# Four row blocks of a weight product in split float32r, and GpSimd taking over subtractions and integer additions of a weight conversion

## The chip, the cores and the metric

One core of one Trainium2 chip. The metric is device time in microseconds (us) of one execution. Before the change three runs took 500.30, 500.75 and 500.87 us, with a median of 500.75. TensorE multiplies matrices into PSUM; VectorE (DVE), ScalarE (ACT) and GpSimd (POOL) work elementwise; SyncE (SP) issues most of the DMAs. Each has its own queue of instructions, kept in order.

## The reference

For 8 batches and 8 heads, `x` has 512 rows of 64 and `state` 32 rows of 64. Attention goes both ways:

```python
scores = scale * x @ state.T          # per head, 512 x 32
xread  = softmax(scores) @ state      # 512 x 64
scores2 = scale * state @ x.T         # 32 x 512
sread  = softmax(scores2) @ x         # 32 x 64
y = concat([xread, sread], rows)      # 544 rows per batch, heads side by side: 512 columns
out = ((y @ w1) * (y @ w2)) @ w3 @ w_out
```

w1 and w2 are 512 x 1024, w3 is 1024 x 1024, w_out 1024 x 512. The weights come as float64, the result is float32.

## The kernel before

**Algebra.** The kernel never forms xread. It multiplies the state by w1 and w2 once per batch ("sw", line 146 through `per_head`) and the transposed softmax by that (`stage1`, line 306), takes the product of the two results (`hidden`), and multiplies by `wo` = w3 @ w_out (`stage2`, through `project`, line 316), which is computed once at the start. Products that must keep float32's accuracy in the float32r type are made from split parts: `split` (lines 93 to 98) makes a high part, a ScalarE copy to float32r, and a low part, a VectorE subtraction; three products (high by low, high by high, low by high) make one.

**The weights.** They lie in DRAM as the bits of float64. `to_f32` (lines 101 to 135) turns one piece of 128 x 1024 into float32 in two halves with a `yield` between them: it loads the 1 MB piece into `raw` (three buffers, line 113); ScalarE makes the value from the high words (line 117) and `ulps`, the rounding part, from the low words (line 125; for the first two pieces VectorE does this, line 121; two buffers); after the `yield` VectorE shifts the bits (line 129) and adds `ulps` as an integer (line 133). There are 20 pieces: eight "chunks" `w34_k` (a row of w_out, 512 columns, and half a row of w3), four rows of w3 (`w3t`, rows 4 to 7; two buffers `w3`), and eight "halves" of w1 and w2 (`w12`, `convert_half`, numbers 0 to 7).

**w3 @ w_out.** Row blocks 0 to 3 of `wo` are accumulated in float32 while the chunks come in (`w34_first`, line 389). Blocks 4 to 7 follow, in float32 too, from the w3 rows (`w34`, line 402): eight matmuls each, each of which is two instructions in the trace. `finish` splits a block into `wo` high and low.

**Order.** Up to `order.close()` (line 461) ScalarE and VectorE keep the order in which the code is written, TensorE and SP always do; behind it a planner orders ScalarE and VectorE. In this first stretch the order is: all eight chunks and w3 rows 4 and 5 with `w34_first`; `load_x(0)`, the scores of batch 0 (line 146 with `x_d`); then block 4, the softmax of batch 0 in steps (`go(softmax)`) between the conversions of halves 0 and 1 (w1_0, w2_0), w3 rows 6 and 7, halves 2 and 3 (w1_1, w2_1); blocks 5 and 6; `sets(0)` (sw of batch 0, first quarter, needs halves 0 and 1); five matmuls of block 7; `sets(1)` (needs halves 2 and 3); the rest of block 7. Then `stage1` of batch 0 runs; halves 4 to 7 are converted beside it, and `sw_steps(0)[2:]` needs them, after the third `stage1`. From there on each batch repeats the same work.

```python
        for k in range(FT + AHEAD):
            run([partial(convert_first, k) if k < FT else partial(convert_w3, k - FT // 2)])
            if k >= AHEAD:
                w34_first(k - AHEAD)
        load_x(0)
```

The rows of w_out in float32 lie in the places of halves 4 to 7 (`places`), so before, a half from 4 on can't be written until block 7 has read them. The low words' name inside `to_f32` is set in line 116:

```python
            high, low = words[:, 1], words[:, 0]
```

GpSimd has nothing in this kernel but four one-element memsets of the launch.

Of the kernel before, what the change touches and what calls it, by code (L numbers as in the profile page):

```python
# [22 lines left out]
F32 = mybir.dt.float32  # L23
# [4 lines left out]
ALU = mybir.AluOpType  # L28
AX = mybir.AxisListType
P = 128  # L30
NF = 512
NW = 1024
AHEAD = 2
LAST = 5
PARTS = {0: (640, 1024), 1: (512, 1024)}
WARM = 15

@with_exitstack
def attn_bilinear_kernel(
# [10 lines left out]
    nc = tc.nc  # L50
    B, _, NT, H, D = x_s.shape
# [4 lines left out]
    FT, DO = w34_k.shape[0], out.shape[2]  # L56
# [30 lines left out]
    def bank():  # L87
        return ps_o.tile([P, NF], F32, name="ps_o")

    def two_banks():  # L90
        return ps_2.tile([P, 2, NF], F32, name="ps_2")

    def split(hi, lo, src):

        return (
            nc.scalar.copy(out=hi, in_=src),  # L96
            nc.vector.tensor_tensor(out=lo, in0=src, in1=hi.bitcast(F32), op=ALU.subtract),  # L97
        )


    def to_f32(pool, src, out, ends=(NW,), loads=(), wout=None):

        raw = pool.tile([P, NW], mybir.dt.int64, name="raw", bufs=3)
        ulps = pool.tile([P, NW], I32, name="ulps", bufs=2)  # L110
        parts = [slice(*ends) for ends in zip((0, *ends), ends)]
        for start, stop in zip((0, *loads), (*loads, NW)):
            nc.sync.dma_start(out=raw[:, start:stop], in_=src[:, start:stop])
        for part in parts:
            words = raw[:, part].bitcast(I32).rearrange("p (n k) -> p k n", k=2)
            high, low = words[:, 1], words[:, 0]
            nc.scalar.activation(  # L117
                out=out[:, part], in_=high.bitcast(F32), func=AF.Prelu, scale=2.0**-112, alpha=-(2.0**32)
            )
            if len(parts) > 1:  # L120
                nc.vector.tensor_scalar(
                    out=ulps[:, part], in0=low.bitcast(U32), scalar1=2.0**-29, scalar2=None, op0=ALU.mult
                )
            else:
                nc.scalar.activation(out=ulps[:, part], in_=low.bitcast(U32), func=AF.Copy, scale=2.0**-29)  # L125
        yield
        for part in parts:
            bits = out[:, part].bitcast(I32)
            nc.vector.tensor_scalar(out=bits, in0=bits, scalar1=3, scalar2=None, op0=ALU.logical_shift_left)
            for dest, start, stop in ((wout, 0, DO), (out, DO, NW)) if wout is not None else ((out, 0, NW),):  # L130
                piece = slice(max(start, part.start), min(stop, part.stop))
                if piece.start < piece.stop:
                    nc.vector.tensor_tensor(  # L133
                        out=dest[:, piece].bitcast(I32), in0=out[:, piece].bitcast(I32), in1=ulps[:, piece], op=ALU.add
                    )

# [37 lines left out]
    def attention_steps(b):  # L174
# [3 lines left out]
        def scores():  # L178
# [6 lines left out]
            s1 = work_tile()  # L185
            nc.vector.transpose(out=flat(s1), in_=flat(ps))

            m2 = att.tile([P, KT], F32, name="m2")
            nc.vector.tensor_reduce(out=m2, in_=ps, axis=AX.X, op=ALU.max)
            nc.vector.tensor_scalar_mul(m2, m2, -SCALE)  # L190
# [3 lines left out]
            for kt in range(KT):  # L194
# [65 lines left out]
    def sw_pair():  # L260
        return [main.tile([P, KT, NF], F32R, name=f"sw_{part}", bufs=2 * HALF) for part in ("hi", "lo")]
# [32 lines left out]
    def new_g():  # L294
        return [main.tile([P, NF], F32R, name=f"g_{part}", bufs=FT) for part in ("hi", "lo")]
# [37 lines left out]
    reads = {}  # L333
# [21 lines left out]
    def run(steps):  # L355
        for step in steps:
            for _ in step() or ():
                pass
# [12 lines left out]
    with tc.tile_pool(name="pro", bufs=2) as pro:  # L371
# [7 lines left out]
        def finish(i):  # L379
            split(wo["hi"][:, i], wo["lo"][:, i], w34_ps[i][:, :DO])  # L380

        def convert_first(k):
            ends = PARTS.get(k, (NW,))
            return to_f32(pro, w34_k[k], chunks[k], ends, (), wout=w_out[k])

        def w34_first(k):

            for i in range(FT // 2):
                nc.tensor.matmul(  # L389
                    w34_ps[i][:, :DO], chunks[k][:, DO + i * P:DO + (i + 1) * P], w_out[k],  # L390
                    start=(k == 0), stop=(k == FT - 1),
                )

        def convert_w3(i):
            w3s[i] = pro.tile([P, NW], F32, name="w3", bufs=2)
            return to_f32(pro, w3t[i - FT // 2], w3s[i])

        def w34(i, ks=range(FT)):
            if ks[0] == 0:
                w34_ps[i] = bank()  # L400
            for k in ks:
                nc.tensor.matmul(  # L402
                    w34_ps[i][:, :DO], w3s[i][:, k * P:(k + 1) * P], w_out[k], start=(k == 0), stop=(k == FT - 1)
                )

        def convert_half(n):

            return to_f32(pro, w12[n], places[n])

        def sets(quarter):  # L410
            for i in range(2):
                sw_quarter(0, quarter, i)
# [9 lines left out]
                    project(acc[tt], gs, tt, ft)  # L422

        order = ctx.enter_context(ExitStack())
        order.enter_context(tc.manual_schedule(engines={mybir.EngineType.Activation, mybir.EngineType.DVE}))
        pair = two_banks()
        w34_ps.update(enumerate([bank(), bank(), pair[:, 0], pair[:, 1]]))
        for k in range(FT + AHEAD):
            run([partial(convert_first, k) if k < FT else partial(convert_w3, k - FT // 2)])
            if k >= AHEAD:  # L430
                w34_first(k - AHEAD)
        load_x(0)
        scores, reads[0], _ = attention_steps(0)
        softmax = scores()
        next(softmax)
        finish(0)
        finish(1)
        split(wo["hi"][:, 2:4], wo["lo"][:, 2:4], pair[:, :, :DO])
        w34(4)

        w1_0, w2_0, w1_1, w2_1 = map(convert_half, range(4))
        go = lambda steps: next(steps, None)
        w3_6 = convert_w3(6)
        go(w1_0), go(softmax), go(w1_0)
        finish(4)
        go(w2_0), go(w3_6), go(softmax), go(w3_6)
        w34(5)
        go(softmax)
        go(w2_0)
        finish(5)  # L450
        w3_7 = convert_w3(7)
        go(w3_7), go(w3_7), go(w1_1), go(w1_1), go(w2_1), go(w2_1)
# [118 lines left out]
```

## Time and profile before

| | us |
|---|---|
| median of three runs | 500.75 |
| span of the profiled execution | 498.4 |
| around that span, against the median | 2.35 |
| TensorE busy | 492.3 |
| VectorE busy | 285.7 |
| ScalarE busy | 219.3 |
| GpSimd busy | 0.2 |

The profiled execution has no time of its own beside its span; the runs' median stands for it. A row of a group reads: line, engine, operation, output <- inputs, shapes, count, then busy time and mean of one in ns, then idle time ahead of them and what ended it. A row of the order of time reads: start, length, engine, line, operation, and in brackets the idle time before it and its releaser. A row of the chain reads: start, length, engine, tile and line.

### The profile page before, as it was taken

What the parts mean: (1) busy time and instruction counts of PE and PEld (TensorE: products, weight loads), DVE (VectorE), ACT (ScalarE), POOL (GpSimd) and SP (SyncE); (2) the same over time, 40 slices, a digit from 0 to 9 for tenths busy, and PEclk for the clock granted to TensorE, in tenths of its full rate; (3) what the DMA queues carried; (4) which work ended last, traced back from release to release, by engine and by line L of the source; (5) the groups of instructions that cost most, each with busy time, mean ns of one, the idle gap of its engine ahead of it and who ended that gap; (6) DMA issues with size and microseconds to landing.
All of it is one profiled execution on the core that took longest, in us unless ns stands there. A gap on an engine that the chain in (4) does not pass through costs nothing.

```text
span 498.4 us, 7562 instructions
## 1 busy us (share of the span) xinstructions
PE 492.3 (99%) x3054; PEld 362.8 (73%) x3054; DVE 285.7 (57%) x394; ACT 219.3 (44%) x325; POOL 0.2 (0%) x4
## 2 busy tenths in 40 slices
PE   8999999999999999999999999999999999999996
PEld 6444467767867886788678867886788678888885
DVE  5669896772539343934393539354934493530780
ACT  4777884443444244334333434243424342431650
POOL 0000000000000000000000000000000000000000
PEclk9999999999999999999999999999999999999999
DMA  8996962013400350035003500350035003301001
GB/s 343 364 380 237 364 264 33 11 47 80 181 22 19 79 189 23 20 79 188 21 27 76 185 22 27 77 184 22 26 78 183 22 26 78 93 24 49 21 1 42
DMA packets 52323, 52.41 MB, mean 105 GB/s; under 512 B 42304, under 2 KB 43328, under 8 KB 47680
## 3 DMA queue, kind: packets, MB, share of 16 engines
q1 hardware_dynamic: 47488, 43.27, 26.3%
q10 hardware_dynamic: 4800, 8.65, 4.6%
q8 instruction: 24, 0.39, 0.3%
q14 instruction: 11, 0.09, 0.1%
HBM read 38.27 MB, written 8.91 MB: 95 GB/s over the span
## 4 chain that ended last, share of the span: by engine, by line
PE 95%; DVE 2%; ACT 2%; DMA 1%; issue 0%; DVEq 0%
PE ps_o L316 38%; PE ps L306 35%; PE ps L146 7%; PE ps L507 3%; PE ps_o L402 3%; PE ps_o L389 3%; PE ps L389 3%; PE ps L508 2%; PE ps_o L242 1%; DMA raw<-in_w_k_dram 1%; ACT ulps L125 0%; ACT w_sb L117 0%; ACT wo_hi L96 0%; DVE w L133 0%; DVE work L204 0%; DVE wo_lo L97 0%
## 5 line engine op out<-in xcount | busy, mean ns | idle before, releaser
L316 PE MATMUL ps_o<-wo_lo,g_hi 128*128 128x512 f32 x272 | 107.0, 394 | 0.0
L316 PE MATMUL ps_o<-wo_hi,g_hi 128*128 128x512 f32 x272 | 106.0, 390 | 0.0
L316 PE MATMUL ps_o<-wo_hi,g_lo 128*128 128x512 f32 x272 | 105.9, 389 | 0.0
L306 PE MATMUL ps<-at_lo,sw_hi 128*128 128x512 f32 x256 | 100.1, 391 | 0.0
L306 PE MATMUL ps<-at_hi,sw_lo 128*128 128x512 f32 x256 | 99.6, 389 | 0.0
L306 PE MATMUL ps<-at_hi,sw_hi 128*128 128x512 f32 x256 | 99.6, 389 | 0.0
L291 DVE TENSOR_TENSOR tmp<-tmp,ps 128x512 f32<-128x512 f32 x64 | 43.9, 687 | 77.0 <-ACT tmp L290 76.9
L97 DVE TENSOR_TENSOR g_lo<-tmp,g_hi 128x512 fp32r<-128x512 f32 (+1 forms) x72 | 47.5, 661 | 41.7 <-ACT g_hi L96 41.6
L96 ACT CAST g_hi<-tmp 128x512 fp32r<-128x512 f32 (+1 forms) x72 | 43.1, 599 | 53.6 <-DVE tmp L291 48.8
L290 ACT COPY tmp<-ps 128x512 f32<-128x512 f32 x64 | 37.7, 589 | 62.8 <-PE ps L306 52.2
L316 PEld LDWEIGHTS ps_o<-wo_lo,g_hi 128*128 128x128 f32 x272 | 51.0, 188 | 18.0 <-issue 7.5
L316 PEld LDWEIGHTS ps_o<-wo_hi,g_lo 128*128 128x128 f32 x272 | 51.1, 188 | 10.8
L316 PEld LDWEIGHTS ps_o<-wo_hi,g_hi 128*128 128x128 f32 x272 | 51.1, 188 | 10.3
L97 DVE TENSOR_TENSOR sw_lo<-ps,sw_hi 128x1024 fp32r<-128x1024 f32 (+1 forms) x34 | 38.4, 1155 | 32.8 <-ACT sw_hi L96 32.8
L306 PEld LDWEIGHTS ps<-at_lo,sw_hi 128*128 128x128 f32 x256 | 48.1, 188 | 10.9 <-issue 1.1
L306 PEld LDWEIGHTS ps<-at_hi,sw_hi 128*128 128x128 f32 x256 | 48.1, 188 | 10.2 <-issue 0.2
L306 PEld LDWEIGHTS ps<-at_hi,sw_lo 128*128 128x128 f32 x256 | 48.1, 188 | 10.0
L329 ACT COPY tmp<-ps_o 128x512 f32<-128x512 f32 x34 | 19.8, 583 | 76.1 <-PE ps_o L316 76.1
L96 ACT CAST sw_hi<-ps 128x1024 fp32r<-128x1024 f32 (+1 forms) x34 | 31.7, 967 | 14.3 <-PE ps L146 14.2
L146 PE MATMUL ps<-w_sb,st 64*32 64x512 f32 (+1 forms) x544 | 31.6, 572 | 0.0
L402 PE MATMUL ps_o<-w_sb,w 128*128 128x512 f32 x64 | 28.5, 599 | 0.1
L402 PEld LDWEIGHTS ps_o<-w_sb,w 128*128 128x128 f32 x64 | 11.8, 190 | 15.9 <-issue 13.8
(65 smaller groups left out, 417.9 us busy)
## 6 DMA issues: line engine op xcount, KB each, us to landing
raw<-in_w_k_dram SPq DMA_DIRECT2D x8, 1024.0 KB, 6.6
x_d<-in_x_d_dram SPq DMA_DIRECT2D x8, 1024.0 KB, 7.1
raw<-in_w_dram SPq DMA_DIRECT2D x8, 1024.0 KB, 6.3
x_s<-in_x_s_dram SPq DMA_DIRECT2D x8, 1024.0 KB, 5.4
out_dram<-tmp ACTq DMA_DIRECT2D x32, 256.0 KB, 2.0
raw<-in_w3t_dram SPq DMA_DIRECT2D x4, 1024.0 KB, 7.2
a_t<-work SPq DMA_DIRECT2D x96, 32.0 KB, 1.9
sread<-turned SPq DMA_DIRECT2D x128, 4.0 KB, 1.7
```

The costliest lines, as they stand in the source:

```text
L96: nc.scalar.copy(out=hi, in_=src),
L97: nc.vector.tensor_tensor(out=lo, in0=src, in1=hi.bitcast(F32), op=ALU.subtract),
L146: nc.tensor.matmul(ps[j * NS:(j + 1) * NS, q], sts[b][rows, j], moving(rows, j), start=True, stop=True)
L290: nc.scalar.copy(out=a_sb[:, :n], in_=ps[:, 0, :n])
L291: nc.vector.tensor_tensor(out=a_sb[:, :n], in0=a_sb[:, :n], in1=ps[:, 1, :n], op=ALU.mult)
L306: nc.tensor.matmul(ps[:, i], w[:, kt, c:c + P], a[:, kt], start=(k == 0), stop=(k == 3 * KT - 1))
L316: nc.tensor.matmul(ps[:, :DO], g, wo[w][:, ft, :], start=(ft == 0 and k == 0), stop=(ft == FT - 1 and k == 2))
L329: stored[:] = [nc.scalar.copy(out=o, in_=ps[:, :DO])]
L389: nc.tensor.matmul(w34_ps[i][:, :DO], chunks[k][:, DO + i * P:DO + (i + 1) * P], w_out[k], start=(k == 0), stop=(k == FT - 1),)
L402: nc.tensor.matmul(w34_ps[i][:, :DO], w3s[i][:, k * P:(k + 1) * P], w_out[k], start=(k == 0), stop=(k == FT - 1))
L507: nc.tensor.matmul(ps[:, i], wh[:, ks], sr[:, kt], start=(kt == 0), stop=False)
L508: nc.tensor.matmul(ps[:, i, :n], wl[:, ks], sr[:, kt, 1], start=False, stop=(kt == NP - 1))
```

## The change

- Blocks 4 to 7 of w3 @ w_out are computed in float32r from split parts: `split_w_out` and `split_w3` make the high parts on ScalarE and the low parts on GpSimd; `w34` issues 24 matmuls a block, first the 16 with the high part of w3, then the 8 with the low part. The parts of w_out lie in the `g` buffers, those of w3 in the `sw` buffers, both unused at that time.
- Blocks 4 and 5 accumulate in a pair of PSUM banks and are split together.
- The integer additions of all eight halves of w1 and w2 go to GpSimd (`add=nc.gpsimd`).
- `to_f32` has a parameter `low` and a test on it, given by `convert_half`.
- x of batch 0 is loaded behind chunk 4; its scores stand on TensorE behind the fourth `w34_first`, and two more `yield`s let the steps of its softmax stand between the chunks.
- GpSimd keeps the written order in the first stretch too, and that order is new.

```diff
-LAST = 5
+X_BEHIND = 4
-    def to_f32(pool, src, out, ends=(NW,), loads=(), wout=None):
+    def to_f32(pool, src, out, ends=(NW,), loads=(), wout=None, add=nc.vector, low=nc.scalar):
...
-            if len(parts) > 1:
+            if low is nc.vector or len(parts) > 1:
                 nc.vector.tensor_scalar(
                     out=ulps[:, part], in0=low.bitcast(U32), scalar1=2.0**-29, scalar2=None, op0=ALU.mult
                 )
...
-                    nc.vector.tensor_tensor(
+                    add.tensor_tensor(
                         out=dest[:, piece].bitcast(I32), in0=out[:, piece].bitcast(I32), in1=ulps[:, piece], op=ALU.add
                     )
...
             nc.vector.transpose(out=flat(s1), in_=flat(ps))
+            if b == 0:
+                yield
...
+            if b == 0:
+                yield
             J = KT * S // NS
...
+        w_out_parts, w3_parts = {}, {}
+
+        def split_w_out(k):
+            hi, lo = w_out_parts[k] = new_g()
+            nc.scalar.copy(out=hi, in_=w_out[k])
+            nc.gpsimd.tensor_tensor(out=lo, in0=w_out[k], in1=hi.bitcast(F32), op=ALU.subtract)
+
+        def split_w3(i):
+            w3_parts[i] = [t.rearrange("p k f -> p (k f)") for t in sw_pair()]
+            hi, lo = w3_parts[i]
+            nc.scalar.copy(out=hi, in_=w3s[i])
+            nc.gpsimd.tensor_tensor(out=lo, in0=w3s[i], in1=hi.bitcast(F32), op=ALU.subtract)
...
+        def w34_terms(i):
+            hi, lo = w3_parts[i]
+            for k in range(FT):
+                for w, part in ((hi, 1), (hi, 0)):
+                    yield w[:, k * P:(k + 1) * P], w_out_parts[k][part]
+            for k in range(FT):
+                yield lo[:, k * P:(k + 1) * P], w_out_parts[k][0]
+
+        def w34(i, first=0, last=3 * FT):
+            if first == 0:
+                w34_ps[i] = bank() if i > 5 else later[:, i % 2]
+            for n, (w, moved) in enumerate(w34_terms(i)):
+                if first <= n < last:
+                    nc.tensor.matmul(
+                        w34_ps[i][:, :DO], w, moved, start=(n == 0), stop=(n == 3 * FT - 1)
+                    )
...
-            return to_f32(pro, w12[n], places[n])
+            return to_f32(pro, w12[n], places[n], add=nc.gpsimd, low=nc.vector if n < 4 else nc.scalar)
...
+        for k in range(FT):
+            chunk = convert_first(k)
+            go(chunk)
+            if k == X_BEHIND:
+                load_x(0)
+            if k:
+                split_w_out(k - 1)
+            if k == X_BEHIND + 1:
+                w34_first(k - AHEAD)
+                scores, reads[0], _ = attention_steps(0)
+                softmax = scores()
+                go(softmax), go(softmax)
+            elif k >= AHEAD:
+                w34_first(k - AHEAD)
+            if k == X_BEHIND + 2:
+                go(softmax)
+            go(chunk)
+        w34_first(FT - 2)
+        w34_first(FT - 1)
+        w3_4, w3_5, w3_6, w3_7 = map(convert_w3, range(FT // 2, FT))
+        w1_0, w2_0, w1_1, w2_1 = map(convert_half, range(4))
+        go(w3_4)
+        split_w_out(FT - 1)
+        go(softmax)
+        go(w3_4)
+        split_w3(4)
+        later = two_banks()
+        w34(4)
+        go(w3_5), go(softmax), go(w3_5)
         finish(0)
         finish(1)
         split(wo["hi"][:, 2:4], wo["lo"][:, 2:4], pair[:, :, :DO])
+        split_w3(5)
         w34(5)
+        go(w3_6), go(w3_6), go(w3_7)
+        split_w3(6)
+        go(w3_7)
+        go(w1_0), go(w1_0), go(w2_0), go(w2_0)
+        split_w3(7)
+        split(wo["hi"][:, 4:6], wo["lo"][:, 4:6], later[:, :, :DO])
         go(softmax)
+        go(w1_1), go(w1_1), go(w2_1), go(w2_1)
         load_tokens(0)
         w34(6)
+        w34(7, 0, 2 * FT)
         sets(0)
         finish(6)
-        w34(7, range(LAST))
+        w34(7, 2 * FT)
         sets(1)
-        w34(7, range(LAST, FT))
         finish(7)
```

More of the change, by code (lines that the diff above doesn't have):

```diff
@@ L424, in attn_bilinear_kernel @@
         order = ctx.enter_context(ExitStack())
-        order.enter_context(tc.manual_schedule(engines={mybir.EngineType.Activation, mybir.EngineType.DVE}))
+        order.enter_context(tc.manual_schedule(
+            engines={mybir.EngineType.Activation, mybir.EngineType.DVE, mybir.EngineType.Pool}
+        ))
+        go = lambda steps: next(steps, None)
         pair = two_banks()
         w34_ps.update(enumerate([bank(), bank(), pair[:, 0], pair[:, 1]]))
-        for k in range(FT + AHEAD):
-            run([partial(convert_first, k) if k < FT else partial(convert_w3, k - FT // 2)])
-            if k >= AHEAD:
-                w34_first(k - AHEAD)
[L432 to L435, printed above, removed]
+        for k in range(FT):
[6 more added lines that the diff above has]
+            if k == X_BEHIND + 1:
+                w34_first(k - AHEAD)
+                scores, reads[0], _ = attention_steps(0)
[18 more added lines that the diff above has]
+        go(w3_5), go(softmax), go(w3_5)
         finish(0)
```

20 lines of the change are left out of this document (1 added, 19 removed).

## The prediction

> **What bounds the kernel now.** I read the page's first part, then the chain that ended last, then the order of time on single engines in the first 78 us, where every edit lies.
>
> ```profile
> span 498.4 us, 7562 instructions
> PE 492.3 (99%) x3054; PEld 362.8 (73%) x3054; DVE 285.7 (57%) x394; ACT 219.3 (44%) x325; POOL 0.2 (0%) x4
> ```
>
> TensorE (PE) is busy for 99% of the span, so a change pays only by what it takes from TensorE, and costs whatever TensorE then has to wait. The chain of work that ended last, in order of time (start, length, what), shows the stretch that changes:
>
> ```profile
> 35.88 1.02 ACT wo_hi L96
> ...
> 50.84 7.13 PE ps_o L402 x16
> 57.98 1.02 PE ps L146 x32
> 59.00 4.49 PE ps_o L402 x10
> 63.49 1.02 PE ps L146 x32
> 64.52 2.77 PE ps_o L402 x6
> 67.29 8.18 PE ps L306 x36
> 75.47 1.88 PE ps L146 x32
> ...
> 119.45 21.76 PE ps L306 x96
> ```
>
> From 50.84 us the chain runs on TensorE without a break. Two places of it are gates: line 146 at 57.98 and 63.49 (sets(0), sets(1)) needs halves 0 to 3 of w1 and w2 converted, and line 146 at 75.47 needs halves 4 to 7. After 75.47 nothing is changed but order, and that part is TensorE's throughout, so the time moves by as much as the start of that group moves.
>
> How near are the other engines? The windows give, for each stretch: its bounds, its length, busy time and count of PE, weight loads, VectorE (DVE), ScalarE (ACT) and GpSimd (POOL), the granted clock, the share of DMA and GB/s.
>
> ```profile
> 8.00:34.00 26.00, 26.00 (x61) 11.26 (x62) 17.93 (x29) 18.85 (x19) 0.00 (x0) 1.00 0.98 372
> 34.00:72.20 38.20, 38.15 (x172) 17.90 (x171) 35.35 (x44) 30.84 (x39) 0.00 (x0) 1.00 0.81 320
> ```
>
> VectorE is busy for 35.35 of 38.20 us and ScalarE for 30.84. Both end just ahead of the gate:
>
> ```profile
> 71.01 1.15 ACT L125 ACTIVATE ulps<-raw 128x1024 int32<-128x1024 uint32 x1
> 72.03 0.60 ACT L290 COPY tmp<-ps 128x512 f32<-128x512 f32 x1
> ...
> 72.76 1.23 DVE L133 CUSTOM_DVE_ANT_0 w_sb<-w_sb,ulps 128x2048 uint16<-128x2048 uint16 x1
> ```
>
> The last addition of half 7 ends at 72.76 + 1.23 = 73.99, only 1.5 us ahead of 75.47. The conversion is thus a second chain, nearly as long as TensorE's, and it decides what a shorter TensorE is worth.
>
> **The change part by part.** *TensorE.* Four rows of w3 @ w_out go from float32 to three float32r products.
>
> ```profile
> 36.80 21.18 PE L402 MATMUL ps_o<-w_sb,w 128*128 128x512 f32 x48
> ```
>
> That is 48 instructions, and with the 10 and 6 of the chain 64, in 21.18 + 4.49 + 2.77 = 28.4 us. In their place stand 4 x 24 = 96 float32r matmuls of the shape of line 306, of which the chain has 96 in 21.76 us. **Removed: 28.4 - 21.8 = 6.6 us.** Were nothing else late, the gate at 75.47 would be reached at 68.9. Batch 0's scores on TensorE (16 matmuls, about 1.0 us) only move.
>
> *ScalarE.* It gets eight copies of w_out rows and four of w3 rows, and gives back next to nothing.
>
> ```profile
> L125 ACT ACTIVATE ulps<-raw 128x1024 int32<-128x1024 uint32 x11 | 12.7, 1156 | 0.0
> L96 ACT CAST wo_hi<-ps_o 128x512 fp32r<-128x512 f32 x6 | 3.4, 586 | 0.0
> L196 ACT ACTIVATE e<-ps,m 128x512 f32<-128x512 f32 x2 | 1.4, 684 | 1.6 <-DVE m L190 1.6
> L207 ACT ACTIVATE work<-work 128x1024 f32<-128x1024 f32 x1 | 1.1, 1061 | 0.9 <-DVE work L204 0.9
> L96 ACT CAST at_hi<-work 128x1024 fp32r<-128x1024 f32 x1 | 1.0, 1047 | 3.3 <-DVE work L220 3.3
> L96 ACT CAST wo_hi<-ps 128x1024 fp32r<-128x1024 f32 x1 | 1.0, 1013 | 0.8 <-PE ps L389 0.8
> ```
>
> A copy of 512 costs 3.4 / 6 = 0.57, one of 1024 1.0 us: 8 x 0.57 + 4 x 1.0 = 8.6 us more on ScalarE. The diff also hands the low words of halves 0 to 3 to VectorE by a parameter `low`. But line 116, which the diff leaves, gives the name `low` to the low words in each part before the test `low is nc.vector` is reached. So the test is false, and the 4 x 12.7 / 11 = 4.6 us of those line-125 operations stay on ScalarE. What this says of the title's low parts touches only these; the low parts of the float32r splits do go to GpSimd.
>
> *Before 34 us* ScalarE has 26.00 - 18.85 = 7.2 us idle; seven of the copies and the two exponentials of scores2 (4.0 + 1.4 = 5.4 us) fit in. The 1 MB load of x_d goes ahead of chunks 5 to 9 in SP's queue: at 372 GB/s it puts each off by 2.8 us. In VectorE's queue the transpose of the scores (1.24 us) now stands ahead of chunk 5's shift and waits for TensorE; chunk 5 to 7's additions and TensorE's first half wait behind it. Chunk 7 is ready at 28.35 and wanted at 32.25, and 1.0 us later with the scores in front:
>
> ```profile
> 27.06 1.29 DVE L133 CUSTOM_DVE_ANT_0 w_sb<-w_sb,ulps 128x1024 uint16<-128x1024 uint16 x2 [0.37 <-ACT ulps L125]
> ...
> 32.25 1.88 PE L389 MATMUL ps_o<-w_sb 128*128 128x512 f32 x4
> ```
>
> Slack 3.9 + 1.0 = 4.9 against 2.8 + 1.2 + 1.2 (a reduction) = 5.2 us. I cost it at nothing; the early lead covers it, and without cover it is 0.3 us.
>
> *From 34 us on ScalarE*: 30.84 - 1.4 (exponentials gone ahead) + 4.0 + 0.6 = 34.0 us of work. Without a wait it ends at 68.0, with the waits of before less the exponentials' (38.20 - 30.84 - 1.6 = 5.8) at 73.8.
>
> *GpSimd.* No operation of this size stands in the trace of before; its four instructions are memsets of one element:
>
> ```profile
> L556 POOL MEMSET const-float32-1.0<- 128x1 f32 x1 | 0.1, 100 | 0.0
> ```
>
> The nearest rows are VectorE's groups from 48 to 75.5 us:
>
> ```profile
> L97 DVE TENSOR_TENSOR at_lo<-work,at_hi 128x1024 fp32r<-128x1024 f32 x1 | 1.2, 1225 | 1.1 <-ACT at_hi L96 1.1
> L97 DVE TENSOR_TENSOR g_lo<-tmp,g_hi 128x512 fp32r<-128x512 f32 x1 | 0.7, 693 | 0.1
> L129 DVE TENSOR_SCALAR w_sb<-w_sb 128x1024 int32<-128x1024 int32 x7 | 4.8, 686 | 0.0
> ```
>
> Low end: GpSimd is as fast as VectorE, 1.2 us for 1024. High end: it reads its operands one after the other and waits for one VectorE operation besides, 2.5 + 1.2 = 3.7 us. From the two VectorE rows an operation has 0.16 us of start and 0.53 us for 512 elements; two passes over 1024 are 0.16 + 4 x 0.53 = **2.3 us**, over 512 1.2 us. I take these, since two inputs on one path are the plainest reason for a slower engine; both ends stay for the range. The Trainium skill, "GPSIMD Engine Reference", section 3.1 "Elementwise — side-by-side cycle accounting", has 4497 ns against VectorE's 2293 for an addition of 2048 elements: an estimate by that ratio is 2.4 us and a sum 1.3 us higher than the one below; no run here shows it.
>
> GpSimd gets, from 34 us on, one low part of w_out (1.2), four of w3 and eight integer additions: 1.2 + 12 x 2.3 = 28.8 us. VectorE loses eight additions, 8 x 1.23 = 9.8 us. New waits: ScalarE's low words of a half need the `ulps` buffer that GpSimd's addition two halves back has to leave (two buffers), and all of ScalarE's later splits are queued behind; the conversion of w3 row 6 (two `w3` buffers) waits in the same way for GpSimd's low part of row 4. The sums of rows 4 and 5 move to the third pair of PSUM banks, and sets(0) takes the first pair, which the copy at 35.88 leaves 20 us ahead of need: no cost.
>
> *Do the two engines run side by side?* This is the term that decides. The shift of line 129 takes 0.69 us for 1024 elements where a two-operand subtraction takes 1.23: it runs at double rate, with one operand. Both kinds so draw two streams at a time from SBUF. If GpSimd reads over the second of those paths, it and these VectorE operations take turns. From 34 us VectorE still has 12 shifts (8.3), four additions for w3 (4.9), the subtraction, product and low part of the softmax (3.7) and two g_lo (1.4): 18.3 us. **Taking turns: 34.0 + 28.8 + 18.3 = 81.1 us** for half 7, against the 75.4 at which the gate opens now: +5.7 us, and the 6.6 us on TensorE become waits ahead of line 146. At 2.0 us an operation it is +2.0, at 2.7 +10.7, at the high end of 3.7 +23, at 1.2 nothing is lost by it.
>
> The Trainium skill, "SBUF — State Buffer", section "SBUF: two separate sides", says that the port pair is an exclusive lock held for a whole instruction, against VectorE operations in a two-port mode or with two SBUF inputs; it speaks against this change. No row of before has both engines at work, so the trace neither agrees nor disagrees yet.
>
> **Forecast**, taking turns: the span goes from 498.4 to 504.1, and the median 500.75, which has 2.35 us more around that span, to **506.4 us**.
>
> **The rivals.** *Side by side, ScalarE last.* ScalarE ends half 7 at 73.8, GpSimd adds 2.3 us: 76.1 against 75.4, +0.7: 501.4 us. For it: GpSimd's own 28.8 us fit into 38. Against it: nothing but the argument on the paths. Spread 499.7 to 503.
>
> *Faster: the waits of ScalarE close.* Of its 7.4 us of waits in the window 3.3 are for one transpose (line 220) behind other work on VectorE, which now has eight additions less. If all close and the engines run side by side, half 7 is done at 68.0 + 2.3 = 70.3 and the gate opens 5.1 us earlier; if half of them close, 73.2: 2.2 us earlier, 498.5 us. It decides as soon as half 7 is added before 75.4 minus 1, so with a GpSimd operation below 2.3 us and under 4 us of ScalarE waits. Against it: in the new order the low part of w3 row 7 stands between the additions of halves 1 and 2, and the transpose of at behind the split of wo rows 4 and 5. Should my reading of `low` be wrong, ScalarE loses 4.6 us and this case is the likely one: about 497.
>
> *The edit does nothing for the end:* the gains on TensorE are eaten in the first half by late chunks and stay even there, within 1 us of before. That lies inside the side-by-side case.
>
> **How the numbers follow.** Taking turns 0.55, all of it slower by over 0.2%; side by side with ScalarE last 0.27 (same 0.17, slower 0.07, faster 0.03); faster 0.18. That is faster 0.21, same 0.17, slower 0.62; 0.2%, 1.0 us, is about what a measurement of this kernel can tell from no change. Cases of both signs hold chances, so: taking turns by itself spans 502.8 (2.0 us an operation) to 511 (2.7 us). The range goes from 499.0, leaving out most of the faster case, 0.12, to 509.5, leaving out 0.08.
>
> **What would show it.** The step on TensorE is right if 96 line-402 or like matmuls take about 21.8 us. Taking turns shows as GpSimd operations of 1024 well over 2.3 us, or VectorE's shift and addition rows lengthened beyond 0.69 and 1.23, and line 146 waiting for GpSimd at sets(1) and at the gate. Side by side shows as unstretched rows and as ScalarE idle for nothing. `low` is read right if the `ulps` group of line 125 on ScalarE still counts 18. I am wrong if stage1 of batch 0 starts by 62 and the gate opens before 74.

## Result and profile after

Four runs of the changed kernel have a median of 517.92 us (517.35 to 518.63), four of the kernel before beside them 500.81 us. The ratio is 1.0345, with a 95% interval of 1.033 to 1.036: 17.1 us slower, where 506.4 us was forecast and 509.5 us was the end of the range.

The lines of the helpers have moved: line 306 of before is now 310 (`stage1`), 316 is 320 (`project`), 389 is 406 (`w34_first`), 402 is 429 (`w34`). The high parts of the new splits stand in lines 390 (w_out) and 396 (w3), the low parts in 391 and 397.

The page's first part, of the changed kernel:

```profile
span 515.8 us, 7647 instructions
PE 493.0 (96%) x3086; PEld 370.5 (72%) x3086; DVE 293.7 (57%) x385; ACT 226.3 (44%) x336; POOL 41.2 (8%) x24
```

TensorE was busy for 99% of the span before, and is now for 96%: the span grew by 515.8 - 498.4 = 17.4 us, and nearly all of it is TensorE waiting. Where, the chain that ended last shows (changed kernel; start, length, what):

```profile
23.36 1.10 PE ps L146 x16
...
63.74 2.69 DVE at_lo L97
66.43 0.61 DVE w_sb L129
...
69.82 2.35 POOL w_sb L133
...
72.22 0.99 PE ps L146 x16
73.21 4.19 PE ps L310 x12
...
79.71 2.37 DVE g_lo L97
...
83.97 1.77 DVE g_lo L97
...
88.18 2.88 POOLq L614
91.06 0.04 issue
91.10 1.96 PE ps L146 x16
93.06 4.49 PE ps_o L320 x12
97.55 5.44 PE ps L310 x24
102.99 2.72 PE ps_o L320 x12
```

Before, the chain ran on TensorE without a break from 50.84 us. Now it leaves TensorE at 24.46 and, but for one group of line 146 and some of `stage1`, comes back for good only at 91.10. `stage1` of batch 0 starts at 73.21 instead of 67.29, 5.9 us later. The gate is line 146 behind it. Before, its two groups of 16 matmuls (halves 4 and 5, then 6 and 7) ran in one piece; the chain of before from there:

```profile
75.47 1.88 PE ps L146 x32
77.35 2.94 PE ps_o L316 x12
80.29 5.44 PE ps L306 x24
```

Now the first group has run ahead, and the second opens at 91.10, 15.6 us behind the 75.47 of before. From there to the next `stage1` the old kernel took 1.88 + 2.94 = 4.82 us for 44 matmuls, the changed one 1.96 + 4.49 = 6.45 us for 28, another 1.6 us. The two make 17.3 us (80.29 against 97.55) of the 17.4.

The windows of the changed kernel give the same stretches as those shown of before (busy time of PE, weight loads, DVE, ACT, POOL, then the granted clock):

```profile
8.00:34.00 26.00, 24.98 (x71) 10.22 (x72) 21.39 (x29) 19.91 (x26) 8.97 (x7) 1.00 0.88 357
34.00:72.20 38.20, 30.58 (x155) 21.09 (x153) 33.19 (x31) 28.55 (x32) 22.02 (x10) 0.96 0.70 269
```

From 34 us on no engine is full any more: VectorE 33.19 of 38.20 (35.35 before), ScalarE 28.55 (30.84), TensorE 30.58 (38.15). Three engines that each have slack and a TensorE that waits mean that they wait for one another. The view of waits of the changed kernel up to 110 us says for what (engine, what waited, releaser: sum, times, longest):

```profile
POOL sw_lo L397 <- ACT sw_hi L396: 12.3, 3, 4.8
PE ps L146 <- POOL w_sb L133: 11.1, 4, 4.6
...
POOL w_sb L133 <- ACT ulps L125: 4.6, 2, 3.3
...
POOL w_sb L133 <- DVE w_sb L129: 3.9, 3, 1.9
```

TensorE waits 11.1 us for GpSimd's additions, as the prediction's signs had it. But GpSimd itself waits: 12.3 us for ScalarE's copies of w3, 4.6 us for the low words, 3.9 us for VectorE's shifts.

**Do the two engines take turns?** GpSimd's operations of the changed kernel, grouped, and some of them in order of time:

```profile
L133 POOL TENSOR_TENSOR w_sb<-w_sb,ulps 128x1024 int32<-128x1024 int32 x8 | 20.0, 2513 | 11.5 <-ACT ulps L125 4.6 <-DVE w_sb L129 3.9 <-ACT g_hi L96 3.0
L391 POOL TENSOR_TENSOR g_lo<-w_sb,g_hi 128x512 fp32r<-128x512 f32 x8 | 10.9, 1363 | 25.9 <-ACT g_hi L390 25.9
L397 POOL TENSOR_TENSOR sw_lo<-w,sw_hi 128x1024 fp32r<-128x1024 f32 x4 | 10.1, 2532 | 12.3 <-ACT sw_hi L396 12.3
```
```profile
41.43 2.40 POOL L397 TENSOR_TENSOR sw_lo<-w,sw_hi 128x1024 fp32r<-128x1024 f32 x1 [4.20 <-ACT sw_hi L396]
48.64 2.42 POOL L397 TENSOR_TENSOR sw_lo<-w,sw_hi 128x1024 fp32r<-128x1024 f32 x1 [4.81 <-ACT sw_hi L396]
57.94 5.06 POOL L133 TENSOR_TENSOR w_sb<-w_sb,ulps 128x1024 int32<-128x1024 int32 x2 [0.73 <-DVE w_sb L129]
62.94 2.41 POOL L397 TENSOR_TENSOR sw_lo<-w,sw_hi 128x1024 fp32r<-128x1024 f32 x1
```

Some of VectorE's operations beside these, by the changed kernel's order of time:

```profile
41.70 2.16 DVE L217 TENSOR_SCALAR sum<-sum 128x32 f32<-128x32 f32 x1
...
48.59 1.21 DVE L97 TENSOR_TENSOR wo_lo<-ps,wo_hi 128x1024 fp32r<-128x1024 f32 x1
49.72 1.88 DVE L129 TENSOR_SCALAR w<-w 128x1024 int32<-128x1024 int32 x1
...
61.39 1.23 DVE L224 STREAM_TRANSPOSE work<-work 128x1024 f32<-128x1024 f32 x1
63.74 2.69 DVE L97 TENSOR_TENSOR at_lo<-work,at_hi 128x1024 fp32r<-128x1024 f32 x1 [1.11 <-ACT at_hi L96]
```

And the first of them before the change:

```profile
46.99 0.18 DVE L213 TENSOR_SCALAR sum<-sum 128x32 f32<-128x32 f32 x1
```

They do. An operation on 32 elements takes 2.16 us instead of 0.18: it ends at 43.86, 0.03 us after GpSimd's (41.43 + 2.40). `at_lo` takes 2.69 instead of 1.23 and ends 1.08 us after GpSimd's. The shift at 49.72 takes 1.88 instead of 0.69. The low part that reads PSUM keeps its 1.21 us with GpSimd at work all along, and so does the transpose at 61.39, which reads one operand in SBUF, with its 1.23. So in these rows a VectorE operation with two operands in SBUF, or with one at double rate (the shift's 0.69 us against the transpose's 1.23 for 1024 elements), that comes second waits for GpSimd's operation to end; the others don't. The wait counts as busy time of VectorE. The Trainium skill, "SBUF — State Buffer", section "SBUF: two separate sides", has the port pair as an exclusive lock for a whole instruction, not a split of bandwidth; these rows agree.

**TensorE's clock after a stall.** Windows of the changed kernel, around its waits (the granted clock is the third from the end):

```profile
39.00:41.50 2.50, 0.00 (x1) 0.03 (x1) 2.42 (x4) 1.60 (x3) 0.07 (x1) 1.00 0.22 92
41.50:45.00 3.50, 3.50 (x9) 2.75 (x10) 3.40 (x4) 3.50 (x5) 2.33 (x1) 0.53 0.29 37
...
73.20:75.40 2.20, 2.20 (x6) 1.76 (x6) 1.40 (x3) 2.13 (x4) 0.00 (x0) 0.50 0.00 0
...
86.50:91.00 4.50, 0.00 (x0) 0.00 (x0) 3.48 (x5) 1.56 (x3) 2.79 (x1) 0.50 0.19 31
91.00:95.00 4.00, 3.90 (x21) 1.85 (x22) 0.72 (x1) 1.01 (x1) 0.05 (x1) 0.50 0.27 43
```

A wait can cost more than its own length: after each of these TensorE ran for 2 to 5 us at half its clock. At the gate the clock had fallen already: windows cut finer show it at half from 86.1 us, behind a wait of 2.4 us and just ahead of the longest one (86.5 to 91.1), until 96.3. Against the rows of before, the 28 matmuls behind the gate took some 2.6 us more for it (1.96 instead of half of 1.88, 4.49 instead of 2.94); as 16 of the 44 had run ahead, 1.6 of that is left in the time. The Trainium skill, "TensorE: Matmul & The Clock Gate", section "What's actually happening", gives half the clock after an idle window of about 3.4 us; here a stall of 2.5 us, at 39.0, was followed by half the clock from 41.7 to 45.1.

### The profile page after: what moved, and what is told of

Read it like the earlier page. It is cut to its first block, busy times and chain, and to the rows that moved or that the text cites. A ratio compares the mean times of both kernels' runs of the same rounds, so it can differ in the third digit from the quotient of the medians.

```text
span 515.8 us, 7647 instructions
## 1 busy us (share of the span) xinstructions
PE 493.0 (96%) x3086; PEld 370.5 (72%) x3086; DVE 293.7 (57%) x385; ACT 226.3 (44%) x336; POOL 41.2 (8%) x24
## 4 chain that ended last, share of the span: by engine, by line
PE 85%; DVE 7%; ACT 4%; POOL 1%; DMA 1%; issue 1%; POOLq 1%; DVEq 0%; ACTq 0%
PE ps_o L320 37%; PE ps L310 33%; PE ps L146 7%; PE ps L554 3%; PE ps L555 1%; PE ps_o L246 1%; DVE w_sb L133 1%; PE ps_o L406 1%; ACT ulps L125 1%; PE ps L406 1%; DMA raw<-in_w_k_dram 1%; DVE w_sb L129 1%; DVE g_lo L97 1%; ACT w_sb L117 1%; ACT sw_hi L396 1%
## 5 line engine op out<-in xcount | busy, mean ns | idle before, releaser
L97 DVE TENSOR_TENSOR g_lo<-tmp,g_hi 128x512 fp32r<-128x512 f32 (+1 forms) x72 | 50.3, 699 | 42.3 <-ACT g_hi L96 42.2
L320 PEld LDWEIGHTS ps_o<-wo_hi,g_hi 128*128 128x128 f32 x272 | 51.5, 189 | 10.4
L310 PEld LDWEIGHTS ps<-at_lo,sw_hi 128*128 128x128 f32 x256 | 48.4, 189 | 11.5 <-issue 0.8
L146 PE MATMUL ps<-w_sb,st 64*32 64x512 f32 (+1 forms) x544 | 33.4, 593 | 11.1 <-POOL w_sb L133 11.1
L146 PEld LDWEIGHTS ps<-w_sb,st 64*32 64x32 f32 x544 | 7.4, 106 | 25.7 <-POOL w_sb L133 13.5
L554 PE MATMUL ps<-grp_sr,grp_z 128*128 128x512 f32 x64 | 22.6, 399 | 0.0
```

The costliest lines, as they stand in the source:

```text
L146: nc.tensor.matmul(ps[j * NS:(j + 1) * NS, q], sts[b][rows, j], moving(rows, j), start=True, stop=True)
L310: nc.tensor.matmul(ps[:, i], w[:, kt, c:c + P], a[:, kt], start=(k == 0), stop=(k == 3 * KT - 1))
L320: nc.tensor.matmul(ps[:, :DO], g, wo[w][:, ft, :], start=(ft == 0 and k == 0), stop=(ft == FT - 1 and k == 2))
L554: nc.tensor.matmul(ps[:, i], wh[:, ks], sr[:, kt], start=(kt == 0), stop=False)
```

## The experiments

All are edits of the changed kernel, except one of the kernel before. The expectations name their theories by letters. A: the loss is GpSimd and VectorE taking turns. B: ScalarE's copies and a full VectorE, in the written order, are the loss wherever the new work is done; B': a low part costs its place in the chain, whoever makes it. C: most of it arises behind `sets(1)`, with halves 4 to 7. D: behind the first stretch the planner puts `stage1`'s copies between the late halves; E: the written order. O, N, V and L are told in their expectations. All results, with the time at which the second group of line 146 behind the start of `stage1` opens (the gate; in the kernel before and in before_light_chain both groups run in one piece, whose start stands there, and the second begins some 0.9 us later):

| kernel | us | ratio to before, 95% | gate |
|---|---|---|---|
| before | 500.8 | | 75.5 |
| changed | 517.9 | 1.033 to 1.036 | 91.1 |
| no_gpsimd_work | 502.3 | 1.001 to 1.004 | 76.8 |
| gpsimd_lows_alone | 507.6 | 1.008 to 1.017 | 82.9 |
| gpsimd_adds_alone | 512.8 | 1.020 to 1.026 | 86.0 |
| all_adds_vector | 515.5 | 1.025 to 1.033 | 89.3 |
| late_adds_vector | 514.1 | 1.022 to 1.030 | 88.8 |
| lows_vector | 520.1 | 1.034 to 1.042 | 93.4 |
| all_on_vector | 515.0 | 1.025 to 1.031 | 89.5 |
| low_words_vector | 520.8 | 1.037 to 1.043 | 94.2 |
| adds_vector_no_lows | 506.3 | 1.007 to 1.013 | 80.7 |
| fewer_copies | 501.6 | 0.999 to 1.003 | 75.9 |
| late_halves_in_written_order | 516.3 | 1.027 to 1.033 | 89.9 |
| late_halves_written_no_lows | 506.7 | 1.008 to 1.014 | 80.6 |
| order_alone | 510.0 | 1.017 to 1.021 | 83.8 |
| scores_behind_first_half | 518.0 | 1.033 to 1.036 | 92.3 |
| light_chain | 497.5 | 0.992 to 0.995 | 73.6 |
| before_light_chain | 500.4 | 0.998 to 1.000 | 75.4 |

The gate accounts for the time nearly throughout: every kernel ends 424 to 427 us behind it, mostly the longer where the matmuls behind it ran at half the clock.

### GpSimd's work taken away, and by parts

```diff
-            nc.gpsimd.tensor_tensor(out=lo, in0=w_out[k], in1=hi.bitcast(F32), op=ALU.subtract)
+            w_out_parts[k] = [hi, hi]
...
-                if piece.start < piece.stop:
+                if piece.start < piece.stop and add is nc.vector:
```

The first edit (and the same for w3) takes the low parts out, the second the eight additions of the halves; no_gpsimd_work has both, the others one each.

> Left out: the low parts made on GpSimd (the high part is used in their place) and the integer additions of all eight halves; TensorE and ScalarE keep every instruction. Theory A (GpSimd and VectorE take turns at SBUF, and that is the loss): the gate at line 146 opens as in the side-by-side rival, less GpSimd's last addition, at 73.8 us or before, so about 499 us, 497 to 503. Theory B (the written order and ScalarE's twelve copies are the loss, whatever GpSimd costs): most of the 17.1 us stays, 510 us or more.

> Left out: the integer additions of all eight halves. The low parts stay on GpSimd. With all GpSimd work gone the time was 502.3 us, with all of it 517.9: 15.6 us. Theory A (what GpSimd holds SBUF for counts wherever it falls): the lows are 21.0 of GpSimd's 41.0 busy us, so about half of it comes back, 510 us, 508.5 to 511.5. Theory C (most is lost behind sets(1), where only additions stand): 506 us or less.

> Left out: the twelve low parts (the high part is used in their place). The eight additions stay on GpSimd. Theory A: half of the 15.6 us comes back, about 510 us. Theory C: most of the loss stays, 512 us or more.

Without GpSimd's work 502.3 us; with the low parts alone +5.3, with the additions alone +10.5, with both +15.6. The two add up. The additions alone came out as theory C had them (512 or more), the low parts alone between what A and C gave. GpSimd's work carries the loss; but as these kernels leave the work out altogether, they can't tell a slow engine or a blocked one from the work as such. They also give the TensorE term in undisturbed form. Windows of no_gpsimd_work, the matmuls of line 429 alone:

```profile
34.00:76.00 42.00, 22.35 (x96) 17.87 (x96) 1.00 0.76 292
```

96 matmuls in 22.35 us, against 28.4 us for the 64 instructions before: 6.1 us less. And still 502.3 us: TensorE's gain isn't seen in the time even with GpSimd idle.

### The same work on VectorE

```diff
-            return to_f32(pro, w12[n], places[n], add=nc.gpsimd, low=nc.vector if n < 4 else nc.scalar)
+            return to_f32(pro, w12[n], places[n])
...
-            nc.gpsimd.tensor_tensor(out=lo, in0=w_out[k], in1=hi.bitcast(F32), op=ALU.subtract)
+            nc.vector.tensor_tensor(out=lo, in0=w_out[k], in1=hi.bitcast(F32), op=ALU.subtract)
```

all_adds_vector has the first edit, late_adds_vector the first for halves 4 to 7 alone, lows_vector the second (for w3 too), all_on_vector both.

> All eight integer additions go back to VectorE; the low parts stay on GpSimd. Theory A: as with the late additions back, and ahead of sets(1) VectorE does 4 x 1.23 = 4.9 us where GpSimd held SBUF for 4 x 2.4 = 9.6: 501.5 to 506 us. Theory B: VectorE, busy for 93% before, has the whole work again and ScalarE the copies: 510 us or more.

> Only the additions of halves 4 to 7 go back to VectorE. In the changed kernel stage 1 of batch 0 starts 5.9 us late (73.21 against 67.29) and the gate opens 15.7 us late (91.10 against 75.4), so 9.7 us are lost between, and some 1.8 us more on TensorE at the lower clock behind the last stall. Theory A: these 11.5 us come back, about 506.4 us, 505 to 509. Theory B: within 2 us of 517.9.

> The low parts of w_out and w3 go to VectorE; the eight additions stay on GpSimd. Theory A taken as a plain sum: GpSimd holds SBUF 8 x 1.27 + 4 x 2.4 = 19.8 us less, VectorE 8 x 0.69 + 4 x 1.23 = 10.4 us more, so 9.4 us come back: about 508.5. Theory B (what counts is the longest chain through engines that each keep their order, and VectorE's queue stands in it): 10.4 us more in VectorE's queue, so slower than 517.9, about 523.

> Nothing left out and nothing on GpSimd: the eight additions and the twelve low parts are on VectorE. Theory A (taking turns is what makes it slow): without turns VectorE pays 8 x 0.69 + 4 x 1.23 = 10.4 us in its own queue against the 21.0 of GpSimd's lows, so less than the 515.5 with the lows on GpSimd, about 510. Theory B' (a low part costs its place in the chain ScalarE, VectorE, TensorE, whoever makes it): 506.3 + 10.4 = 516.7, 514 to 519.

This is where theory A as the whole story falls. In all_on_vector GpSimd does nothing and no lock can be held, and the time is 515.0 us: 2.9 of the 17.1 us come back. The additions on VectorE bring 2.4 us, which is B's side; those of halves 4 to 7 alone bring 3.8, which neither A nor B gave, so the four early additions are 1.4 us better off on GpSimd. The low parts on VectorE, with the additions left on GpSimd, cost 2.2 more, in B's direction but less than its 523. With nothing on GpSimd, then, the loss is the work's place in the chain, as B' has it. In all_on_vector VectorE is busy for 33.28 us from 34.0 to 72.2, against 33.19 in the changed kernel, where it has fewer operations and waits for GpSimd in them. What moving work to GpSimd costs in all, its slower operations, VectorE's waits and VectorE's relief together, is seen in pairs that differ in nothing but the engine: eight additions, +2.4 us with low parts on GpSimd (515.5 to 517.9), +5.1 with low parts on VectorE (515.0 to 520.1), +6.6 without low parts (506.3 to 512.8); twelve low parts, 0.5 us between the engines, though GpSimd takes 21 us for them.

One more edit in this group makes the test on `low` true, as its caller seems to mean it:

```diff
-    def to_f32(pool, src, out, ends=(NW,), loads=(), wout=None, add=nc.vector, low=nc.scalar):
+    def to_f32(pool, src, out, ends=(NW,), loads=(), wout=None, add=nc.vector, low_on=nc.scalar):
...
-            if low is nc.vector or len(parts) > 1:
+            if low_on is nc.vector or len(parts) > 1:
```

> The changed kernel with the parameter renamed so that the test is true: VectorE makes the low words of halves 0 to 3. Theory B (ScalarE last): 4 x 1.05 us less on ScalarE, about 513.7. Theory A (GpSimd and VectorE are the bound and take turns): four double-rate operations of 0.69 us more on VectorE, 517.9 to 521.

The low words of halves 0 to 3 are then made by VectorE, and the time is 520.8, 2.9 us worse, inside theory A's 517.9 to 521. Where it goes is seen in ScalarE's waits (low_words_vector, from 30 to 95 us):

```profile
ACT at_hi L96 <- DVE work L224: 5.6, 1, 5.6
```

In the changed kernel that wait for VectorE's transpose was 2.4 us. ScalarE is relieved of four operations, and waits instead.

### Without low parts, and without most copies

```diff
+            if k:
+                w_out_parts[k] = w_out_parts[0]
+                return
...
+            if i > 4:
+                w3_parts[i] = w3_parts[4]
+                return
```

Both kernels have the additions on VectorE and no low parts; fewer_copies has this edit in `split_w_out` and `split_w3` besides.

> Left out: the twelve low parts. The eight additions are on VectorE, so GpSimd does nothing and VectorE has what it had before, ScalarE its work of before and 8.6 us of copies. Theory B (VectorE and ScalarE were full, so that the additions cost as much there): 505 us or more. Theory A (GpSimd's presence is the loss): within 2 us of the 502.3 without any of this work.

> As the kernel with the additions on VectorE and without the low parts (506.3 us), and ScalarE's copies of w_out rows 1 to 7 and of w3 rows 5 to 7 are left out too (row 0's and row 4's parts stand for them), 7 x 0.6 + 3 x 1.0 = 7.2 us of ScalarE. Theory B (ScalarE's copies keep this kernel above the one before): the gate opens up to 5.2 us earlier, 501.5 us or less. Theory E (the written order with its waits between ScalarE and VectorE does): 504.5 us or more.

The ten copies cost 506.3 - 501.6 = 4.7 us, the twelve low parts 515.5 - 506.3 = 9.2 us. Taken off in this order (another order shifts the shares: without additions the low parts cost 5.3), the account of the 17.1 us is: 0.8 for the float32r blocks in the new order with two copies left, 4.7 for the other ten copies, 9.2 for the low parts, 2.4 for the additions on GpSimd. At the first of these steps TensorE's 6 us are already gone. A part of that is the clock: the profiled execution ran at half of it behind the gate, and the two of the eight whose mean clock was 1.0 took 499.8 us, 1.0 less than before. Why so little of the 6 us is left, the window of fewer_copies shows:

```profile
34.00:72.20 38.20, 36.91 (x213) 26.65 (x218) 35.11 (x44) 32.26 (x37) 0.00 (x0) 1.00 0.85 324
```

VectorE is as full as before the change (35.11 against 35.35) and ScalarE fuller, while TensorE begins to wait. In the view of waits of fewer_copies from 34 to 96 us that is one row:

```profile
PE ps L146 <- DVE w_sb L133: 3.0, 1, 3.0
```

The gate opens when half 7 is added, and that ends at 75.84 there (74.69 + 1.15, by the chain), not sooner than the 73.99 of before.

### The order

```diff
+        run([partial(convert_half, n) for n in range(4, 2 * QT)])
         order.close()
...
-                run([partial(convert_half, n) for n in range(4, 2 * QT)])
```

This puts the conversions of halves 4 to 7 into the written order, ahead of `stage1`'s copies; the second kernel has adds_vector_no_lows besides.

> Nothing left out; the conversions of halves 4 to 7 are written ahead of stage 1, so ScalarE's and VectorE's queues have them ahead of the copies of stage 1's results, which wait for TensorE. In the changed kernel the planner puts those copies between them (ScalarE idle ahead of them at 73.3, 77.4, 83.3 and 87.5 us). Theory D (that circle of waits is what is lost behind sets(1)): ScalarE ends four halves at 2.1 us each, the gate opens at about 85 and not 91.1, and the time is about 511.5 us, 510 to 513. Theory A (GpSimd's pace sets it alone, four additions at 3.7 us): within 2 us of 517.9.

> As the kernel with the additions on VectorE and without the low parts (506.3 us), with the conversions of halves 4 to 7 written ahead of stage 1. Theory D (stage 1's five copies, 0.52 us apart from the next instruction, and 1.4 us of waits for TensorE stand in ScalarE's queue ahead of half 7): the gate opens 4 us earlier, about 502.3. Otherwise, as with the additions on GpSimd, it is worth under 2 us: 504.5 or more.

1.6 us come back in the first, none in the second (506.7 against 506.3): theory D, which gave some 6 and 4 us, is refuted.

The third part of the change, and the order by itself. order_alone has blocks 4 to 7 in float32 as before, without copies, low parts or GpSimd, in the change's order; scores_behind_first_half is the changed kernel with the scores of batch 0 behind the first half again:

```diff
-            for n, (w, moved) in enumerate(w34_terms(i)):
-                if first <= n < last:
+            for k in range(FT):
+                if first <= 3 * k < last:
```
```diff
-            if k == X_BEHIND:
-                load_x(0)
...
+        load_x(0)
+        scores, reads[0], _ = attention_steps(0)
+        softmax = scores()
+        go(softmax)
```

> The change's order of work (scores of batch 0 inside the first half, steps of its softmax between the chunks, w3 rows and halves written behind one another) with blocks 4 to 7 in float32 as before: no copies, no low parts, all integer additions on VectorE, nothing on GpSimd. TensorE has the 6.6 us again that the change removes. Theory O (the order itself costs; that is why the kernel with neither low parts nor most copies, 501.6 us, gains nothing from 6.6 us less TensorE work): the order delays the conversions by about as much as TensorE was shortened, so that with the float32 blocks back the time is 503 to 508 us. Theory N (the order is neutral; the conversion chain alone, 1.5 us ahead of the gate before the change, holds the gate near 75.5 whatever TensorE does): 500.8 us within 1, with the gate group of line 146 at 75 to 76.5.

> The changed kernel, with x of batch 0 loaded and its scores and softmax placed behind the first half again, as before the change; everything else of the change stays. Theory O (the scores in the first half cost: TensorE waited 3.2 us there and VectorE 2.8 us): the first half ends 2 to 3 us earlier and the time is 514 to 516 us. Theory N (those waits are absorbed, since the chain of ScalarE, VectorE and GpSimd behind the first half holds the gate, and it would have the softmax of batch 0 to do as well): 517.9 us within 1, or up to 521 us, as ScalarE and VectorE have some 5 us more behind the first half.

The moved scores are worth nothing either way: 518.0 against 517.9. The order by itself is 9.2 us slower than before, but by a mechanism that the float32r kernels don't have. ScalarE's waits in order_alone, from 30 to 84 us:

```profile
ACT w L117 <- PE ps L424: 8.8, 2, 4.7
```

In float32, TensorE reads the rows of w3 themselves, out of two buffers; the new order converts rows 6 and 7 directly behind row 5, so ScalarE waits twice for blocks 4 and 5 to be done. Before, halves 0 and 1 stood between. With split parts the copies free the buffers, and this wait isn't there. So theory O's direction came, by more than its 503 to 508 us and for another reason: order_alone doesn't explain why fewer_copies gains nothing.

### A lighter chain

```diff
-                if piece.start < piece.stop:
+                if piece.start < piece.stop and ulp:
...
-            return to_f32(pro, w12[n], places[n])
+            return to_f32(pro, w12[n], places[n], ulp=False)
```

light_chain has this edit on top of fewer_copies, before_light_chain has it on the kernel before. Where `ulp` is false, the operation that makes the low words is left out too.

> As the kernel with neither low parts nor most of the copies (501.6 us: w_out copies from row 1 and w3 copies from row 5 left out, the parts of row 0 and row 4 stand in, additions on VectorE), and besides the low words of the eight halves of w1 and w2 and their integer additions are left out. Per half, ScalarE loses 1.0 us and VectorE 1.2 us. Theory V (ScalarE and VectorE hold the gate, and TensorE's 6.6 us are there for the taking): the gate opens at 69 to 72 us and the time is 494.5 to 497.5 us. Theory L (the loads, or something else that this does not touch, hold the gate): the gate stays above 74 and the time is 499.5 us or more.

> The kernel before the change, with the low words of the eight halves of w1 and w2 and their integer additions left out, the same relief of ScalarE and VectorE. Theory V: TensorE without a break is the bound there, so the relief brings nothing: 500.8 us within 1, gate at 75.5 within 0.5. Rival: the chain is the bound before too, and the time falls by 2 us or more.

The same relief of ScalarE and VectorE takes 4.1 us from fewer_copies (501.6 to 497.5, at the edge of what theory V gave) and 0.5 us from the kernel before. The gate moves by 2.3 of the 4.1 (75.88 to 73.55); the rest is the clock, which behind the gate of light_chain isn't halved (2.93 us for the twelve matmuls of `project`, 4.76 in fewer_copies). The chain of light_chain, in order of time, is TensorE's again:

```profile
38.34 11.20 PE ps L437 x48
49.54 9.07 PE ps_o L437 x40
58.60 1.02 PE ps L148 x32
59.63 2.04 PE ps_o L437 x8
61.66 1.02 PE ps L148 x32
62.69 5.68 PE ps L312 x24
68.37 0.02 issue
68.39 0.60 ACT tmp L296
```

`stage1` (line 312 there) starts at 62.69 instead of 67.29. The gate came at 73.55, not at the 69 to 72 that V gave: behind 68.37 the chain goes through the first set's products and splits (`tmp`, `g_hi`), which this relief doesn't touch, so 3.4 of TensorE's 6 us reach the end. The loads, theory L, weren't touched, and the gate moved below L's 74 all the same.

## Why the prediction missed

- **TensorE, 6.6 us less**: right; 22.35 us instead of 21.8 in no_gpsimd_work. In the changed kernel itself they took 24.25 us, some of them at half clock behind a stall.
- **`low`**: read right. The `ulps` group of line 125 on ScalarE over the whole changed kernel, by the view of groups:

```profile
L125 ACT ACTIVATE ulps<-raw 128x1024 int32<-128x1024 uint32 x18 | 20.7, 1148 | 0.0
```

  But "about 497" for the case that it acts was wrong in sign: 520.8. I took what leaves ScalarE as a gain and forgot that VectorE, 35.35 of 38.20 us full, gets it.
- **GpSimd's price**, 2.3 and 1.2 us: 2.40 and 1.27 undisturbed, 2.51 to 2.53 and 1.36 on average. Right.
- **Before 34 us, at nothing**: wrong, but harmless. TensorE waited there, by the group of its first half in the changed kernel:

```profile
L406 PE MATMUL ps_o<-w_sb 128*128 128x512 f32 x32 | 15.6, 609 | 3.2 <-DVE w_sb L133 3.2
```

  scores_behind_first_half takes the scores away from there and gains nothing.
- **Side by side, ScalarE last; faster**: neither came. The rows above show the lock, and ScalarE's waits didn't close: `at_hi` is at 62.66 instead of 51.98.
- **The failing step is the sum "Taking turns: 34.0 + 28.8 + 18.3 = 81.1 us"**, mis-sized by 10.0 us: the gate opened at 91.10. The turns are there, but the sum took busy times alone, as if GpSimd and VectorE handed over without a gap. Of the 57.1 us from 34.0 to 91.1 GpSimd spent 31.4 in the thirteen operations that begin there (by the view in order of time) and 25.7 outside them, 7.4 us more than the 18.3 that VectorE's turns were given; with 2.6 us more of its own work that is the 10.0.
- **What stood in its place** is a chain of waits. What GpSimd waited for directly is mostly not VectorE: 12.3 us of the 25.7 are waits for ScalarE's copies of w3, 4.6 for low words, 3.9 for shifts, 3.0 for a `g_hi` copy. Each of ScalarE, VectorE and GpSimd keeps its order, and each new piece passes from one to the other (addition, copy, low part, matmul). That their waits add up for this reason is argued from these rows, not shown by a run of its own. Turns do lie further up in the chain that ended last: from 34 us five of its VectorE pieces (`work` of line 208 at 36.37, `sum` of line 217, `at_lo`, two `g_lo`) are together 6.9 us longer than undisturbed. But all_on_vector, with no turns at all and the same work on VectorE, still takes 515.0 us.
- **What the sum left out**: the half clock behind the gate, 1.6 us net. 10.0 + 1.6, and 0.1 on the rest of the span, less the 0.2 us by which the time around the span is smaller (517.92 - 515.8 = 2.1 against 2.35), are the 11.5 us between 506.4 and 517.9.
- **Half 7's lead over the gate, "only 1.5 us"**: read too short. The 16 matmuls that need halves 6 and 7 come behind the 16 for halves 4 and 5, at about 76.4, so half 7, added at 73.99, had 2.4 us. By the same reading 81.1 us would have meant +4.7 rather than +5.7.
- **The idea underneath**, that the conversion is "a second chain, nearly as long as TensorE's", was right, and should have been carried further. It ends 2.4 us ahead of the matmuls that need it, so most of what is put on it shows, and little of what is taken from TensorE alone. fewer_copies, light_chain and before_light_chain show three sides of that: less TensorE (and two more copies, in the new order) 501.6, less of both 497.5, less chain alone 500.4.

**Left open.** What the lock alone costs isn't separated from the slower engine: the same eight additions cost 2.4 to 6.6 us more on GpSimd, depending on where the low parts are. The float32r blocks in the order of before weren't run, so the new order's part in fewer_copies isn't known. No kernel that computes the whole product and is faster than before came out of this; light_chain leaves work out. Making the split parts where VectorE and ScalarE have slack wasn't tried.

## What to carry to other kernels

When one engine is full and a second chain ends just ahead of the place where both meet, shortening the first is worth little more than that lead, and most of what the shortening puts on the chain is paid (ten copies of 7.2 us cost 4.7 here, twelve low parts of 10.4 us on VectorE 8.7): count the added copies and low parts before the saved matmuls. For a chain through several in-order engines, follow the pieces one after the other; the sum of busy times gave only a lower end here, 10 us short. And work moved from VectorE to GpSimd isn't off VectorE: an operation of 0.18 us can take 2.16.

## What the runs showed of the hardware

- The lock hits the smallest operations hardest: 128 x 32 elements, 2.16 us instead of 0.18, because it lasts as long as GpSimd's operation. VectorE's subtraction with PSUM as an input (1.21 us) and its transpose in SBUF (1.23 us) ran beside GpSimd unstretched.
- Integer addition and float32 subtraction of 1024 elements take GpSimd the same 2.40 us, 512 take 1.27.
- A TensorE stall of 2.5 us was followed by half the granted clock over most of the next 3.5 us (0.53). At the gate half the clock, granted from 86.1 to 96.3 us, made 28 matmuls some 2.6 us longer.
